# Agent attention with a PReLU MLP: the first batch's scores with agents as rows, in halves of TensorE's columns

## Chip, cores and metric

The kernel runs on one core of a Trainium2 chip. The metric is device time in microseconds; each kernel is run several times and the median is given. The engines are TensorE (PE in the profile), VectorE (DVE), ScalarE (ACT), GpSimd (POOL) and SyncE (SP), which issues the DMAs here.

## The reference

Agent attention for 2 batches of 12480 rows and 128 channels, with 49 agents, then an MLP of width 2048 with a learned slope for negative values:

```python
scale = 1.0 / np.sqrt(q.shape[-1])
def sm(a, b):
    s = scale * (a @ b.transpose(0, 2, 1))
    s = s - s.max(-1, keepdims=True)
    e = np.exp(s)
    return e / (e.sum(-1, keepdims=True) + 1e-09)
agent_v = sm(agents, k) @ v            # 49 x 128 per batch
x = sm(q, agents) @ agent_v            # 12480 x 128 per batch
h = x @ w_in                           # 24960 x 2048
out = (np.maximum(h, 0) + alpha * np.minimum(h, 0)) @ w_out
```

Everything is fp32. q, k and agents are drawn with a spread of 0.8, w_in and w_out arrive as fp64 and are put together from their two words on the chip.

## The kernel before

The work is in two parts. A first part handles batch 0's keys and values, w_in, w_out and the first queries. Then a long loop of 52 groups of 480 rows, 8 steps each, computes h (`g1`), its ReLU halves on ACT and DVE, and the output (`g2`), with batch 1's keys and values worked in between at fixed steps. `agent_v` is never formed for the loop: it is multiplied into w_in first (`fold_tasks`), and the loop multiplies query weights by that product (`sab`).

In the first part the keys come in blocks of 512, 25 in all, two blocks to a load. Per block `k_transpose_pe` transposes four 128x128 pieces on TensorE (tile ktp) and ACT copies them (kt). `k_logits` takes each piece as weights and the 49 agents as moving data, so scores lie with keys as rows, 49 columns per piece (kl); ACT copies them to an SBUF tile s (`k_take`, line 426). In five spans of blocks (`CUTS`) DVE takes the maximum over keys (`k_max_keys`, line 445); two transposes on TensorE turn it into one maximum per agent and spread it to all rows (`k_max_rows`, `k_max_spread`). Then `k_exp_a` (line 529) subtracts it on DVE or GpSimd, `k_exp` takes the exponential on ACT and `k_av` multiplies weights and values (av, line 561), with a column of ones next to each 128 values for the denominator. `k_factors` and `k_gather` bring the five spans to one maximum. The fold follows: `t1` divides by the denominator, `t2` transposes (avt), `ta` multiplies by w_in (a_ps) and splits the product into two parts.

What an engine does when is written out by step numbers: a plan from step to functions, walked in order, so each engine has one fixed list. Loads go out on SP's queue in the order of a sorted list, each when one of the 14 buffers of a ring is free; K, V, w_in and w_out share that ring. The first queries' chain (`q_transpose` to `q_split`; q_max, line 798, is a GpSimd all-reduce) is put among these steps by `CHAIN_0`, their loads by `Q_LOADS`. `stoke` issues dummy matmuls. `narrow` joins the fp64 words on DVE, partly on GpSimd, and `narrow_wo` makes the two parts of (1 - alpha) w_out.

## Time and profile before

| | |
|---|---|
| median of 3 runs | 1011.86 us (1010.86 to 1012.33) |
| the profiled execution's own time | 1012.12 us |
| its span | 1010.0 us |
| TensorE busy over the span | 994.7 us, 98% |
| DVE, ACT, GpSimd busy | 841.8, 631.0, 111.7 us |
| first matmul of the long loop | 84.72 us |

Times inside a trace count from the first instruction of the span; the profiled execution is 2.12 us longer than its span. Busy shares over the whole span hide the first part, so the table by stage matters more: 0 to 8.38 is the start, up to 73.30 the blocks, up to 79.87 the way to the fold, up to 84.72 the fold, and then the loop. An fp32 matmul appears as two records (two passes), an fp32r matmul as one; a shape as 64*128 means that only half of the array's rows are used, and two such matmuls on different halves stand side by side.

### The profile page before, as it was taken

The page shows a single profiled execution, that of the slowest core. Times are in us where ns is not written, and L with a number is a line of the kernel's source. Part 1 is how long each engine was busy: PE and PEld are TensorE (multiplying, and loading weights), DVE is VectorE, ACT ScalarE, POOL GpSimd, SP SyncE. Part 2 cuts the span into 40 slices and gives each one's busy share as a digit, 9 for nine tenths or more (in the row PEclk, how much of TensorE's full clock was granted, in tenths as well). Part 3 has the DMA queues.
Part 4 walks back from the last instruction along what each step waited for, and adds up shares of the span by engine and source line. Part 5 has one row for each costly group of instructions (what it writes and reads, how often), then busy time and mean ns, then how long its engine had stood idle before and what let it go on. Part 6 is the DMA issues. An engine that isn't in the chain of part 4 may idle for free.

```text
span 1010.0 us, 22035 instructions
## 1 busy us (share of the span) xinstructions
PE 994.7 (98%) x9154; PEld 898.9 (89%) x9154; DVE 841.8 (83%) x1058; ACT 631.0 (62%) x803; POOL 111.7 (11%) x106
## 2 busy tenths in 40 slices
PE   9998999999999999999999999999999999999997
PEld 7885899999998999999988888888888888888886
DVE  5966689889889999999997887888788878887775
ACT  5655555556557677677765666666666665666653
POOL 2430110110110110111011011101110111011100
PEclk9998999999999999999999999999999999999999
DMA  9970344444423432342322122122222222221101
GB/s 329 239 169 1 62 86 74 87 85 67 78 56 67 83 78 56 72 92 64 69 49 52 35 41 51 39 51 41 51 43 48 41 50 46 45 41 32 40 12 30
DMA packets 295764, 69.52 MB, mean 69 GB/s; under 512 B 263071, under 2 KB 290289, under 8 KB 295665
## 3 DMA queue, kind: packets, MB, share of 16 engines
q1 hardware_dynamic: 294673, 68.00, 32.4%
q8 instruction: 71, 1.16, 0.5%
q14 instruction: 28, 0.23, 0.1%
q10 hardware_dynamic: 992, 0.12, 0.1%
HBM read 42.59 MB, written 12.78 MB: 55 GB/s over the span
## 4 chain that ended last, share of the span: by engine, by line
PE 95%; DVE 2%; ACT 1%; POOL 0%; issue 0%; DVEq 0%; ACTq 0%; POOLq 0%
PE acc L894 55%; PE h L872 27%; PE kl L406 4%; PE lg L770 2%; PE acc L905 1%; PE av L594 1%; PE qsum L827 1%; PE av L561 1%; PE a_ps L656 1%; PE ktp L374 1%; PE warm L179 1%; PE lin_ps L723 0%; POOL qm L798 0%; DVE mx L445 0%; PE stoke L179 0%
## 5 line engine op out<-in xcount | busy, mean ns | idle before, releaser
L879 DVE SCALAR_TENSOR_TENSOR rl<-h,rh 128x960 fp32r<-128x960 f32 x416 | 478.8, 1151 | 128.3 <-ACT rh L878 125.6
L878 ACT ACTIVATE rh<-h 128x960 fp32r<-128x960 f32 x416 | 404.3, 972 | 276.5 <-PE h L872 269.4
L872 PE MATMUL h<-qmh,sab 64*128 64x480 f32 x1664 | 377.4, 378 | 0.5 <-DVE rl L879 0.5
L894 PE MATMUL acc<-rh,wl 64*128 64x480 f32 x1664 | 377.4, 379 | 0.0
L894 PE MATMUL acc<-rh,wh 64*128 64x480 f32 x1664 | 375.2, 377 | 0.0
L894 PE MATMUL acc<-rl,wh 64*128 64x480 f32 x1664 | 294.6, 378 | 0.0
L872 PEld LDWEIGHTS h<-qmh,sab 64*128 64x128 f32 x1664 | 233.1, 185 | 20.0 <-DVE rl L879 2.0
L894 PEld LDWEIGHTS acc<-rh,wl 64*128 64x128 f32 x1664 | 231.3, 184 | 18.1 <-issue 2.3
L894 PEld LDWEIGHTS acc<-rh,wh 64*128 64x128 f32 x1664 | 232.6, 185 | 16.2
L894 PEld LDWEIGHTS acc<-rl,wh 64*128 64x128 f32 x1664 | 199.7, 184 | 15.2
L872 PE MATMUL h<-qml,sab 64*128 64x480 f32 x832 | 204.1, 378 | 0.0
L798 POOL PARTITION_ALL_REDUCE qm<-qs x26 | 85.7, 3295 | 778.4 <-DVE qs L794 734.3
L872 PEld LDWEIGHTS h<-qml,sab 64*128 64x128 f32 x832 | 117.5, 185 | 7.0
L406 PEld LDWEIGHTS kl<-ag,kt 64*128 64x128 f32 (+2 forms) x588 | 49.3, 188 | 1.6 <-ACT s L535 0.7
L910 ACT COPY os<-acc 128x480 f32<-128x480 f32 x52 | 29.1, 560 | 34.3 <-PE acc L905 34.3
L406 PE MATMUL kl<-ag,kt 64*128 64x49 f32 (+2 forms) x588 | 49.9, 268 | 0.0
L807 ACT ACTIVATE qmh<-qs,padb 128x960 fp32r<-128x960 f32 x26 | 28.5, 1097 | 14.0 <-DVE qs L803 14.0
L911 DVE TENSOR_TENSOR os<-acc,os 128x480 f32<-128x480 f32 x52 | 34.0, 655 | 2.8 <-ACT os L910 2.4
L916 DVE STREAM_TRANSPOSE ot<-os 128x480 f32<-128x480 f32 x52 | 34.8, 669 | 0.0
L803 DVE TENSOR_TENSOR qs<-qs,qm 128x960 f32<-128x960 f32 x26 | 29.9, 1149 | 5.2 <-POOL qm L798 5.2
L921 DVE TENSOR_TENSOR ot<-ot,qr 128x480 f32<-128x480 f32 x52 | 33.7, 648 | 0.1
L794 DVE TENSOR_TENSOR qs<-qs,qw 128x960 f32<-128x960 f32 x26 | 29.9, 1149 | 1.2 <-DMA qw<-qs 1.1
(149 smaller groups left out, 850.6 us busy)
## 6 DMA issues: line engine op xcount, KB each, us to landing
qin<-in_q_dram SPq DMA_DIRECT2D x208, 60.0 KB
out_dram<-ot SPq DMA_DIRECT2D x206, 60.0 KB
qw<-qs SPq DMA_DIRECT2D x50, 240.0 KB
v<-in_v_dram SPq DMA_DIRECT2D x12, 512.0 KB
kb<-in_k_dram SPq DMA_DIRECT2D x96, 64.0 KB
v<-in_v_dram SPq DMA_DIRECT2D x24, 256.0 KB
k<-in_k_dram SPq DMA_DIRECT2D x11, 512.0 KB
win<-in_moe_w_in_dram SPq DMA_DIRECT2D x4, 512.0 KB
```

The lines of the kernel that those rows point to most:

```text
L406: nc.tensor.matmul(d[0:rows, c : c + NA], lhsT=kt[r0:r1, n * rows : (n + 1) * rows], rhs=st[b]["ag"][r0:r1, 0:NA], start=True, stop=True,)
L794: nc.vector.tensor_tensor(out=t, in0=t, in1=gq.pop(("w", k)), op=ALU.add)
L798: nc.gpsimd.partition_all_reduce(flat(t), flat(gq["s", k]), P, ReduceOp.max)
L803: nc.vector.tensor_tensor(out=t, in0=t, in1=gq.pop(("m", k)), op=ALU.subtract)
L872: nc.tensor.matmul(h[:, u, 0:GT], lhsT=w[a][r0:r1, f0 : f0 + P], rhs=x[r0:r1, :], start=n == 0, stop=n == 2,)
L878: nc.scalar.activation(out=rh, in_=h[:, :, 0:GT], func=AF.Relu)
L879: nc.vector.scalar_tensor_tensor(out=rl, in0=h[:, :, 0:GT], scalar=0.0, in1=rh, op0=ALU.max, op1=ALU.subtract)
L894: nc.tensor.matmul(acc[:, i, 0:GT], lhsT=a[r0:r1, 2 * m + u, :], rhs=x[r0:r1, u, :], start=m == 0 and n == 0, stop=False,)
L910: nc.scalar.copy(out=t, in_=acc[:, 0, 0:GT])
L911: nc.vector.tensor_tensor(out=t, in0=acc[:, 1, 0:GT], in1=t, op=ALU.add)
L916: nc.vector.transpose(out=t.rearrange("p t i -> p (t i)"), in_=oo.pop(g))
L921: nc.vector.tensor_tensor(out=t, in0=t, in1=gq.pop(("r", g)).to_broadcast([P, TB, 32]), op=ALU.mult)
```

## The change

Only batch 0's keys and values are worked differently; batch 1 and the loop stay. Keys come in packs of 1024 (a first one of 192 rows, then twelve), each one load; a pack's first 512 keys belong to half 0, the others to half 1. The 64 agent columns (49, padded) are the weights and 512 transposed keys the moving data, so `k_score` writes half 0 to PSUM rows 0 to 63 and half 1 to rows 64 to 127, which are two halves of the array's columns. Now a row is an agent: `k_top` keeps a running maximum per row on DVE, `k_weigh` takes the exponential of 512 scores straight from PSUM with the row sum, and a factor from the last maximum to this one; `k_back` transposes the weights back on TensorE, `k_mix` multiplies them by the values in halves of the columns again, and DVE adds to x with the factor. `k_merge` and `k_share` join the two halves and make the reciprocal of the denominator, which is now put on when the product with w_in is split (`take`). The column of ones, the score tile s, the spans and the GpSimd subtractions go. The ring has 12 buffers instead of 14, of 1024 words per partition instead of 1032. Two of the (1 - alpha) products move to GpSimd, `fold` and its like are made by DVE from the identity, and a small all-reduce on GpSimd (`library`) is called before the first queries'. Step numbers of the w_in and w_out slabs, the dummy matmuls (16 instead of 8), the query loads and the queries' chain are new.

```diff
-CHAIN_0 = (-9, -8, -7, -5, -4, -4, 0, 0, 3, 4, 6, 6)
+CHAIN_0 = (-19, -17, -15, -11, -9, -9, 0, 2, 8, 15, 18, 18)
...
+LAGS = (6, 8, 11, 17)
+LIBRARY_AT = 43
...
-Q_LOADS = (-21, -15)
+Q_LOADS = (-49, 0)
...
+    def library():
+
+        t = p2.tile([P, 1], F32, tag="none", name="none")
+        nc.gpsimd.partition_all_reduce(t, ones[:, 0:1].bitcast(F32), P, ReduceOp.max)
...
+    def load_wide(src, what, p):
+        r0, rows, nb = wide(p)
+        t = p_in.tile([P, RING], F32, tag="in", name=f"{what}w{p}")
+        view = t[0:rows, 0 : 2 * nb * C].rearrange("p (n c) -> p n c", c=C)
+        nc.sync.dma_start(
+            out=view, in_=src[0, r0 : r0 + rows * 2 * nb, :].rearrange("(p n) c -> p n c", p=rows)
+        )
+        kv[what, p] = view
+    def k_turn(p):
+        _, rows, nb = wide(p)
+        src, n = kv.pop(("k", p)), nb * rows
+        t = ps_h.tile([P, 2, 512], F32, tag="h", name=f"ktp{p}")
+        for i in range(2):
+            for j in range(nb):
+                nc.tensor.transpose(
+                    t[:, i, j * rows : (j + 1) * rows], src[:, i * nb + j, :],
+                    ident[0:rows, 0:rows],
+                )
+        kt = p_kt.tile([P, 2, KT], F32, tag="kt", name=f"ktw{p}")[:, :, 0:n]
+        nc.scalar.copy(out=kt, in_=t[:, :, 0:n])
+        kv["kt", p] = kt
+    def k_score(p):
+        kt = kv.pop(("kt", p))
+        n = kt.shape[2]
+        t = ps_a.tile([P, 512], F32, tag="acc", name=f"sc{p}")[:, 0:n]
+        for i, (r0, r1) in enumerate(TILES):
+            nc.tensor.matmul(t[r0:r1, :], lhsT=st[0]["ag"], rhs=kt[:, i, :], start=True, stop=True)
+        kv["sc", p] = t
+    def k_top(p):
+        w, t = st[0], kv["sc", p]
+        red = p2.tile([P, 1], F32, tag="red", name=f"red{p}")
+        nc.vector.tensor_reduce(out=red, in_=t, axis=AX.X, op=ALU.max)
+        if p == 0:
+            for x in ("nm", "den", "kf"):
+                w[x] = per_b.tile([P, NPK], F32, tag=x, name=x, bufs=1)
+            w["x"] = per_b.tile([P, C], F32, tag="xw", name="xw", bufs=1)
+            nc.vector.tensor_scalar(
+                out=w["nm"][:, 0:1], in0=red, scalar1=-SCALE, scalar2=None, op0=ALU.mult
+            )
         else:
+            nc.vector.scalar_tensor_tensor(
+                out=w["nm"][:, p : p + 1], in0=red, scalar=-SCALE, in1=w["nm"][:, p - 1 : p],
+                op0=ALU.mult, op1=ALU.min,
+            )
+    def k_weigh(p):
+        w, t = st[0], kv.pop(("sc", p))
+        e = p_e.tile([P, KT], F32, tag="e", name=f"ew{p}")[:, 0 : t.shape[1]]
+        nm = w["nm"][:, p : p + 1]
+        nc.scalar.activation(
+            out=e, in_=t, func=AF.Exp, bias=nm, scale=SCALE, accum_out=w["den"][:, p : p + 1]
+        )
+        if p:
+            nc.scalar.activation(
+                out=w["kf"][:, p : p + 1], in_=w["nm"][:, p - 1 : p], func=AF.Exp,
+                bias=nm, scale=-1.0,
+            )
+        kv["e", p] = e
+    def k_back(p):
+        _, rows, nb = wide(p)
+        e = kv.pop(("e", p))
+        t = ps_l.tile([P, 512], F32, tag="lg", name=f"etp{p}")
+        for j in range(nb):
+            nc.tensor.transpose(
+                t[0:rows, j * P : (j + 1) * P], e[:, j * rows : (j + 1) * rows], ident
+            )
+        et = p_e.tile([P, UB * P], F32, tag="et", name=f"et{p}")[0:rows, 0 : nb * P]
+        (nc.vector.tensor_copy if BACK_DVE[p] else nc.scalar.copy)(
+            out=et, in_=t[0:rows, 0 : nb * P]
+        )
+        kv["et", p] = et.rearrange("p (n a) -> p n a", a=P)
+    def k_mix(p):
+        w = st[0]
+        _, rows, nb = wide(p)
+        et, src = kv.pop(("et", p)), kv.pop(("v", p))
+        t = ps_k.tile([P, 512], F32, tag="km", name=f"avw{p}")[:, 0:C]
+        for j in range(nb):
+            for i, (r0, r1) in enumerate(TILES):
+                nc.tensor.matmul(
+                    t[r0:r1, :], lhsT=et[:, j, r0:r1], rhs=src[:, i * nb + j, :],
+                    start=j == 0, stop=j == nb - 1,
+                )
+        x = w["x"]
+        if p == 0:
+            nc.vector.tensor_copy(x, t)
+        else:
+            nc.vector.scalar_tensor_tensor(
+                out=x, in0=x, scalar=w["kf"][:, p : p + 1], in1=t, op0=ALU.mult, op1=ALU.add
+            )
+    def k_merge():
+        w = st[0]
+        last = w["nm"][:, NPK - 1 : NPK]
+        top = p2.tile([P, 1], F32, tag="red", name="top")
+        for i, (r0, r1) in enumerate(TILES):
+            o0, o1 = TILES[1 - i]
+            nc.scalar.copy(out=top[r0:r1, :], in_=last[o0:o1, :])
+        nc.vector.tensor_tensor(out=top, in0=top, in1=last, op=ALU.min)
+        f = per_b.tile([P, NPK], F32, tag="kff", name="kff", bufs=1)
+        nc.scalar.activation(out=f, in_=w["nm"], func=AF.Exp, bias=top, scale=-1.0)
+        w["fold"] = per_b.tile([P, P], F32, tag="foldw", name="foldw", bufs=1)
+        nc.vector.tensor_scalar(
+            out=w["fold"], in0=both, scalar1=f[:, NPK - 1 : NPK], scalar2=None, op0=ALU.mult
+        )
+        nc.vector.tensor_tensor(out=f, in0=f, in1=w["den"], op=ALU.mult)
+        den = p2.tile([P, 1], F32, tag="red", name="den_sum")
+        nc.vector.tensor_reduce(out=den, in_=f, axis=AX.X, op=ALU.add)
+        w["den_sum"] = den
+    def k_share():
+        w = st[0]
+        t = ps_l.tile([P, 512], F32, tag="lg", name="den_ps")[:, 0:1]
+        nc.tensor.matmul(t, lhsT=both, rhs=w.pop("den_sum"), start=True, stop=True)
+        rs = w["rs"] = per_b.tile([P, 1], F32, tag="rsw", name="rsw", bufs=1)
+        nc.vector.tensor_scalar(out=rs, in0=t, scalar1=1e-9, scalar2=None, op0=ALU.add)
+        nc.vector.reciprocal(out=rs, in_=rs)
...
+        def take(hi, lo, ps):
+            if b:
+                nc.scalar.copy(out=hi, in_=ps)
+                nc.vector.tensor_tensor(out=lo, in0=ps, in1=hi, op=ALU.subtract)
+            else:
+                rs = w["rs"][:, 0:1]
+                nc.scalar.activation(out=hi, in_=ps, func=AF.Copy, scale=rs)
+                nc.vector.scalar_tensor_tensor(
+                    out=lo, in0=ps, scalar=rs, in1=hi, op0=ALU.mult, op1=ALU.subtract
+                )
...
+        for p in range(NPK):
+            at(4 * p, k_turn, p)
+            loads.append((4 * p + LAGS[3] - V_AHEAD, load_wide, v, "v", p))
+            for n, f in zip(LAGS, ((k_score, k_top), (k_weigh,), (k_back,), (k_mix,))):
+                for g in f:
+                    at(4 * p + n, g, p)
+        q0 = 4 * NPK
+        end = q0 - 4 + LAGS[1]
+        at(end + 1, k_merge)
+        at(end + 2, k_share)
```

On TensorE, in the middle of the first part, two blocks of 512 keys before (ktp transposes, av values, kl scores):

```order
L374 MATMUL ktp0_20_671<-ident_82,k0_20_408 128x128 x4
L561 MATMUL av0_1_648<-v0_4_358,s0_173 49x129 x4
L406 MATMUL kl0_19_690<-ag0_165,kt0_19_643 128x49 x4
L374 MATMUL ktp0_21_696<-ident_82,k0_20_408 128x128 x4
L561 MATMUL av0_1_648<-v0_4_358,s0_173 49x129 x4
L406 MATMUL kl0_20_717<-ag0_165,kt0_20_676 128x49 x4
```

and a pack of 1024 keys now (avw values, sc scores, etp weights back, ktp keys):

```order
L434 MATMUL avw4_555<-vw4_372,et4_483 64x128 x8
L375 MATMUL sc7_569<-ktw7_500,ag0_160 64x512 x2
L417 MATMUL etp6_582<-ident_82,ew6_536 128x128 x4
L361 MATMUL ktp9_597<-ident_82,kw9_406 128x128 x8
L434 MATMUL avw5_610<-vw5_449,et5_531 64x128 x8
L375 MATMUL sc8_633<-ktw8_548,ag0_160 64x512 x2
```

Eight matmuls of 49 columns, eight of 129 and eight transposes have become two matmuls of 512 columns, eight of 128 and twelve transposes, of four different packs; the last two rows begin the next round.

On SP, around the second query load before (qin; k and v are packs of batch 0):

```order
L225 DMA wo_3_468<-in_moe_w_out_dram 128x4x256
L346 DMA k0_22_471<-in_k_dram 128x1024
L740 DMA qin1_486<-in_q_dram 32x15x32 x8
L346 DMA v0_8_495<-in_v_dram 128x8x128
L346 DMA k0_24_502<-in_k_dram 96x256
L346 DMA v0_10_552<-in_v_dram 128x8x128
```

and now, around the first (kw, vw are packs; win and wo are slabs of the weights):

```order
L349 DMA kw3_174<-in_k_dram 128x1024
L761 DMA qin0_176<-in_q_dram 32x15x32 x8
L234 DMA win_3_185<-in_moe_w_in_dram 128x1024
L349 DMA kw4_187<-in_k_dram 128x1024
L349 DMA vw0_189<-in_v_dram 96x256
L243 DMA wo_0_191<-in_moe_w_out_dram 128x4x256
L349 DMA kw5_193<-in_k_dram 128x1024
```

and the second:

```order
L349 DMA vw9_553<-in_v_dram 128x1024
L349 DMA vw10_565<-in_v_dram 128x1024
L349 DMA vw11_608<-in_v_dram 128x1024
L761 DMA qin1_620<-in_q_dram 32x15x32 x8
L349 DMA vw12_629<-in_v_dram 128x1024
L761 DMA qin2_1001<-in_q_dram 32x15x32 x8
```

The first query load has moved ahead of the last w_in slab and the fifth key pack, the second from the middle of the values to just ahead of the last value pack.

On DVE, at the end of the first part, before (x the weighted values, qs and qml the queries' scores and the lower part of their weights, avt the fold):

```order
L803 TENSOR_TENSOR qs0_866<-qs0_866,qm0_910 128x960
L504 COPY kfs0_948<-kf_ps0_942 49x5
L506 TENSOR_SCALAR x0_176<-x0_176,kfs0_948 49x129
L510 SCALAR_TENSOR_TENSOR x0_176<-x0_176,kfs0_948 49x129 x3
L816 TENSOR_TENSOR qml0_966<-qs0_866,qmh0_955 128x960
L573 SCALAR_TENSOR_TENSOR x0_176<-av0_4_937,kfs0_948,x0_176 49x129
L630 TENSOR_SCALAR rs0_1022<-x0_176 49x1
L633 RECIPROCAL rs0_1022<-rs0_1022 49x1
L634 TENSOR_TENSOR x0_176<-x0_176,rs0_1022 49x128
L647 COPY avt0_1028<-avt_ps0_1026 128x128
```

and now (nm the running minimum of negated maxima, top and kff the merge of the halves, rsw the reciprocal, wl a remainder of w_out, xw the weighted values):

```order
L454 TENSOR_TENSOR top_847<-top_847,nm_234 128x1
L458 TENSOR_SCALAR foldw_853<-both_85,kff_851 128x128
L461 TENSOR_TENSOR kff_851<-kff_851,den_235 128x13
L463 TENSOR_REDUCE den_sum_856<-kff_851 128x1
L472 TENSOR_SCALAR rsw_860<-den_ps_858 128x1
L473 RECIPROCAL rsw_860<-rsw_860 128x1
L320 TENSOR_TENSOR wl_97<-part3_788,wh_96 128x512
L824 TENSOR_TENSOR qs0_703<-qs0_703,qm0_824 128x960
L442 SCALAR_TENSOR_TENSOR xw_237<-xw_237,kf_236,avw11_872 128x128
L442 SCALAR_TENSOR_TENSOR xw_237<-xw_237,kf_236,avw12_882 128x128
L837 TENSOR_TENSOR qml0_895<-qs0_703,qmh0_892 128x960
L664 COPY avt0_951<-avt_ps0_949 128x128
```

The queries' subtraction stood ahead of the merge of the spans; now the merge of the halves and the reciprocal stand ahead of it, and the last two additions to x behind it.

## Rows read from the trace of the kernel before

**Rows 1.** Table by stage: us, busy per engine, TensorE's clock, DMA share, GB/s.

```profile
8.38:73.30 64.92, 63.36 (x527) 56.51 (x527) 49.11 (x97) 40.45 (x100) 25.60 (x46) 1.00 0.93 258
73.30:79.87 6.57, 2.19 (x18) 1.75 (x17) 4.54 (x11) 4.25 (x10) 0.78 (x1) 0.95 0.00 0
79.87:84.72 4.85, 4.46 (x6) 1.63 (x6) 1.27 (x3) 0.58 (x1) 0.00 (x0) 0.50 0.00 0
84.72:1010.00 925.28, 918.21 (x8591) 834.46 (x8590) 783.88 (x932) 584.46 (x691) 84.54 (x52) 1.00 0.29 55
```

**Rows 2.** Chain of waits, middle stage: start, duration, what, count.

```profile
13.96 1.23 PE stoke L179 x5
...
21.72 0.83 PE kl L406 x8
...
42.99 0.46 PE ktp L374 x4
43.44 1.02 PE av L561 x8
44.46 1.02 PE kl L406 x8
```

**Rows 3.** Chain of waits from 74 to 93 us.

```profile
74.11 1.17 DVE qs L803
...
75.31 1.10 ACT qmh L807
...
76.49 1.10 ACT qs L812
...
80.67 0.30 DVE avt L647
...
81.02 3.78 PE a_ps L656 x4
...
91.40 1.06 PE a_ps L656 x2
```

**Rows 4.** Timeline of GpSimd: start, duration, operation, idle before.

```profile
71.02 3.06 POOL L798 PARTITION_ALL_REDUCE qm<-qs  x1 [5.94 <-issue]
```

**Rows 5.** Timeline of TensorE, scores of the second batch.

```profile
141.75 1.97 PE L406 MATMUL kl<-ag,kt 64*128 64x49 f32 x31
...
143.55 0.27 PE L406 MATMUL kl<-ag,kt 64*128 64x49 f32 x1
```

**Rows 6.** Groups by line, 0 to 90 us, weight loads: busy us, mean ns.

```profile
L561 PEld LDWEIGHTS av<-v,s 128*49 128x49 f32 x192 | 20.4, 123 | 3.0 <-issue 1.6 <-ACT s L535 0.7 <-ACT aq L203 0.3
```

**Rows 7.** Groups by line, 0 to 90 us, DVE.

```profile
L445 DVE TENSOR_REDUCE mx<-s 128x49 f32<-128x1176 f32 x3 | 6.8, 2260 | 0.0
...
L445 DVE TENSOR_REDUCE mx<-s 128x49 f32<-128x588 f32 x2 | 2.4, 1178 | 0.0
...
L529 DVE TENSOR_TENSOR s<-s,kmax 128x196 f32<-128x196 f32 x6 | 2.1, 358 | 0.0
L663 DVE TENSOR_TENSOR sab<-a_ps,sab 128x512 fp32r<-128x512 f32 x3 | 2.1, 685 | 2.8 <-ACT sab L662 2.8
...
L264 DVE TENSOR_SCALAR scale_win<-mag_win 128x512 uint32<-128x512 uint32 x4 | 1.7, 423 | 0.0
...
L463 DVE TENSOR_REDUCE mcol<-mx_ps 49x1 f32<-49x128 f32 x5 | 1.4, 283 | 0.4 <-PE mx_ps L461 0.4
```

**Rows 8.** Groups by line, 0 to 90 us, ACT and GpSimd.

```profile
L378 ACT COPY kt<-ktp 128x512 f32<-128x512 f32 x24 | 14.1, 589 | 11.7 <-PE ktp L374 11.6
L529 POOL TENSOR_TENSOR s<-s,kmax 128x196 f32<-128x196 f32 x18 | 13.5, 770 | 8.9 <-DVE kmax L472 8.8
```

**Rows 9.** Table by stage, the loads of K and of V.

```profile
2.00:21.00 19.00, 18.12 (x114) 15.23 (x113) 11.11 (x35) 8.07 (x18) 4.04 (x10) 1.00 1.00 356
...
47.00:63.00 16.00, 15.92 (x129) 13.60 (x129) 12.81 (x22) 9.18 (x25) 8.46 (x13) 1.00 1.06 272
```

**Rows 10.** Timeline of SP: the first query load, eight issues.

```profile
21.05 9.35 SPq L740 DMA_DIRECT2D qin<-in_q_dram  x8
```

More of the change, by code (lines that the diff above doesn't have):

```diff
@@ L78 @@
     W = 512
-    N_IN = 14
+    N_IN = 12
     WARM = 13
-    RING = 2 * UB * (C + 1)
+    RING = 2 * UB * C
+    REST = N % (2 * KT)
+    NPK = N // (2 * KT) + 1
     NM = NF // 2
     SCALE = 1.0 / math.sqrt(C)
+    assert 0 < REST <= 2 * P and REST % 2 == 0
     assert N % GT == 0 and N % 64 == 0 and NA <= HALF and C == P and D == P and DFF % W == 0
@@ L112, in blocks, with wide @@
         return u * KT, n // nb, nb
+    def wide(p):
+        if p == 0:
+            return N - REST, REST // 2, 1
+        return (p - 1) * 2 * KT, P, UB
     ident = const.tile([P, P], F32, name="ident")
@@ L133 @@
     st = [
-        dict(rows=2 * NA, cols=2 * C + 2) if b else dict(rows=NA, cols=C + 1) for b in range(B)
+        dict(rows=2 * NA, cols=2 * C + 2) if b else {} for b in range(B)
     ]
@@ L156, in constants @@
         nc.gpsimd.memset(ones.bitcast(F32), 1.0)
-        for t, w in ((fold, HALF), (pair, NA)):
-            nc.gpsimd.memset(t, 0.0)
-            view = t.rearrange("p (h c) -> p h c", h=2)[:, :, 0:NA]
-            for base in (0, -NA):
-                nc.gpsimd.affine_select(
-                    out=view, in_=view, compare_op=ALU.not_equal, fill=1.0,
-                    base=base, pattern=[[0, 2], [-1, NA]], channel_multiplier=1,
-                )
+        for t, w, gap in ((fold, HALF, NA), (pair, NA, NA), (both, HALF, HALF)):
+            rows = t.shape[0]
+            if w > NA:
+                nc.gpsimd.memset(t, 0.0)
+            parts = [ident[0:rows, i : i + NA].unsqueeze(1) for i in (0, gap)]
+            v.tensor_tensor(
+                out=t.rearrange("p (h c) -> p h c", h=2)[:, :, 0:NA],
+                in0=parts[0].to_broadcast([rows, 2, NA]),
+                in1=parts[1].to_broadcast([rows, 2, NA]), op=ALU.add,
+            )
         valid = const.tile([P, 1], F32, name="valid")
@@ L320, in k_begin @@
         st[b]["x"] = per_b.tile(
[L321 removed]
+            [st[b]["rows"], 2, st[b]["cols"]], F32, tag=f"x{b}", name=f"x{b}", bufs=1
         )
[L324 to L325 removed]
     kv = {}
[L329 to L350 removed]
@@ L367, in load_blk @@
         return t
-    def k_transpose_pe(b, u):
-        _, rows, nb = blocks(u)
-        src = kv.pop(("k", b, u))
-        t = ps_h.tile([P, 2, 512], F32, tag="h", name=f"ktp{b}_{u}")[:, 0, 0 : nb * rows]
-        for n in range(nb):
-            nc.tensor.transpose(
-                t[:, n * rows : (n + 1) * rows], src[:, n, 0:C], ident[0:rows, 0:rows]
-            )
-        kt = p_kt.tile([P, KT], F32, tag="kt", name=f"kt{b}_{u}")[:, 0 : nb * rows]
-        nc.scalar.copy(out=kt, in_=t)
-        kv["kt", b, u] = kt
     def load_kb(b, u):
@@ L640, in t2 @@
             w["ps"] = pair_tile(f"avt_ps{b}")[:, 0, :]
-            for i in range(parts):
+            jobs = [(w["x"], w["fold"])] if b == 0 else [
+                (w["x"][:, i * C : (i + 1) * C], fold[0:rows, :]) for i in range(parts)
+            ]
+            for i, (x, f) in enumerate(jobs):
                 nc.tensor.matmul(
-                    w["ps"][:, 0:P], lhsT=w["x"][:, i * C : (i + 1) * C], rhs=fold[0:rows, :],
-                    start=(i == 0), stop=(i == parts - 1),
+                    w["ps"][:, 0:P], lhsT=x, rhs=f, start=i == 0, stop=i == len(jobs) - 1
                 )
@@ L661, in f @@
                     sl = slice(n * W, (n + 1) * W)
-                    nc.scalar.copy(out=w["sa"][:, sl], in_=ps[:, t, :])
-                    nc.vector.tensor_tensor(
-                        out=w["sb"][:, sl], in0=ps[:, t, :], in1=w["sa"][:, sl],
-                        op=ALU.subtract,
-                    )
+                    take(w["sa"][:, sl], w["sb"][:, sl], ps[:, t, :])
             return f
@@ L676, in ts @@
             w["zl"] = per_b.tile([P, D], F32R, tag="zl", name=f"zl{b}")
-            nc.scalar.copy(out=w["zh"], in_=w["z_ps"])
-            nc.vector.tensor_tensor(
-                out=w["zl"], in0=w["z_ps"], in1=w["zh"], op=ALU.subtract
-            )
+            take(w["zh"], w["zl"], w["z_ps"])
         whole = [(0, 1), (2, 3)] if b else [(n,) for n in range(4)]
-        first = [t1, t2] + [ta(*ns) for ns in whole]
+        first = [t1] * b + [t2] + [ta(*ns) for ns in whole]
         rest = [tz, ts]
@@ L996 @@
             at(q0 + j, f, 0)
+        at(LIBRARY_AT, library)
         for n in range(8):
```

222 lines of the change are left out of this document (43 added, 179 removed).

## The prediction

> **What bounds the kernel now.** Begin with the table by stage [rows 1]. From 84.72 us to the end (925.28 us) TensorE is busy 918.21 us at granted clock 1.00: the long loop is TensorE's. The change does not touch it, apart from the first fold in front of it, so I take its length as fixed. What can move is the time at which its first matmul, h of step 0, starts: 84.72 us. Before that stand three stages. From 8.38 to 73.30 the first batch's keys and values are worked off, with TensorE busy 63.36 of 64.92 us, DVE 49.11, ACT 40.45 and the DMA engines at 0.93. From 73.30 to 79.87 TensorE does 2.19 us of work. From 79.87 to 84.72 it runs at clock 0.50, its lower level of 1.2 GHz.
>
> The chain of waits [rows 2] shows the middle stage as TensorE work end to end: per 512 keys four transposes 0.46, scores 1.02 and values 1.02 us, so 5.0 us per 1024 keys; early blocks, without values, have scores of 0.83. So the stage is TensorE's too, though the DMA lane is nearly full. The tail [rows 3] hangs on another lane: GpSimd's maximum over the first queries ends at 74.09, then DVE subtracts, ACT takes two exponentials, and DVE, in its fixed order, comes to the value chain only behind them. GpSimd's maximum itself stood idle 5.94 us with nothing shown as its cause [rows 4].
>
> **The change on TensorE's lane.** A pack is 1024 keys, twelve and a small one.
> Transposes stay: 8 per pack, 0.91 us, 11.1 in all.
> Scores were 16 matmul records of 49 columns per 1024 keys (2.04 or 1.66 us). Now they are two matmuls of 512 columns into column halves, two passes each. A pass of 512 columns took 3.78/4 = 0.945 us at half clock [rows 3], so 0.47 at full: 1.89 us if the halves follow each other, 0.95 if they overlap fully. Passes go out in order (half 0 twice, then half 1 twice), so I allow one pass at each end alone: three slots, 1.4 us.
> Values were 16 records of 129 columns, 2.04 us. Now 16 passes of 128 columns: 2.04 one after the other (0.1275 each), 1.02 overlapped; with one pass alone 1.15.
> New: four transposes back, 0.46 us. Switching between whole array and halves: the a_ps pair at full clock, standing between matmuls in row halves, took 1.06 us against 2 x 0.47 [rows 3], so 0.115 for in and out, once per pack.
> So a pack is 0.91 + 1.4 + 0.46 + 1.15 + 0.1 = 4.0 us, against 5.0.
>
> No row shows column halves. The nearest are row halves: in the second batch, 32 score passes in halves took 143.55 - 141.75 = 1.80 us [rows 5], 0.056 each, where the first batch's whole-array passes took 0.83/8 = 0.104 [rows 2]. Two-pass fp32 matmuls in two halves did overlap. I therefore stand near the overlapped end and keep the serial one for the range.
>
> The Trainium skill's page "TensorEngine Tiling (Array Packing)", Key Properties, has tiles loading weights and multiplying independently, and says that changing the mode drains the engine; by the first the sum stands, and for the second the 0.115 us stands in. Its page "TensorE: Matmul & The Clock Gate", Measured speedup vs the span model, gives column tiles a gain within a few ns of row tiles. But the same page, Part 3, The mechanism, lets a weight load overlap a running matmul only when the row groups differ, and column halves share all rows; that speaks against the change and is the fourth case below. The value rows do not bear it out in the whole array: a pass took 0.1275 us with a weight load of 0.123 us beside it [rows 6].
>
> The lane: 11.1 transposes, 12 x 1.4 + 0.3 = 17.1 scores, 5.6 back, 14.0 values, 1.4 switches, 16 dummy matmuls at 1.23/5 = 0.246 [rows 2] = 3.9, query scores 0.9, small ones 0.4: 54.4 us, against 64.92. Without waiting it runs from 8.4 to 62.8; the last pack's scores, with 4.6 us of work behind them, end at S = 58.2.
>
> **DVE's lane.** Of 49.11 us go the key maxima and what hung on them: 9.1 (3 x 2.260 + 2 x 1.178), ten groups of small operations, the subtractions (2.1) the largest, 8.4 in all, and two 512-wide products moved to GpSimd, 1.4 [rows 7]. New are 13 row maxima over 512 scores. Their bounds are the 128-column maximum, 0.283, and the strided 588-element one, 1.178; I take the 512-wide operation on PSUM, 0.685. That makes 8.9; running minima 13 x 0.15, updates of x 12 x 0.34, three copies back 2.0, and the query subtraction that falls into the stage now, 1.2. Sum 47 us: no longer much shorter than TensorE's 54. In its list up to nine 512-wide operations stand between two row maxima: in the longest group, around the fifth pack, five at 0.423 and four at 0.685 [rows 7], with the maximum and small ones 6.4 us. That exceeds a pack's 4.0 by 2.4, and the exponential, the transpose back and TensorE wait for it. I add 2.4: S = 60.5. Without any idle DVE alone would put S at 55.5; with the share it is filled now (49.11/64.92 = 0.76) at 64.
>
> ACT, at 40.45 of 64.92 us, has room. Its 24 key copies of 0.589 [rows 8] become half as many of twice the width; copies of scores give way to copies of the weights turned back (ten of 512, 0.59 each), and 24 exponentials of 196 columns to 13 of up to 512. Even a third more would leave it under TensorE. GpSimd loses 13.5 us of subtractions [rows 8]. So neither decides.
>
> **Loads.** K ran at 356 GB/s; values, in 512 B pieces since a column of ones stood beside each row, at 272 [rows 9]. Now they have no such column. 14.9 MB at 356 are 42 us; two query loads, 0.49 MB each in 128 B pieces, I estimate at a third of that rate, 4 us each: about 50 us after the first issue, under 60. But SP took 9.35 us to issue a query load [rows 10]. The first now stands before the last slab of w_in and the fifth key pack: SP comes to that pack at about 14 us, and TensorE wants it, by its lane, at 19. The second stands before the last value pack. SP comes to it when a weight slab is done on DVE, some 16 us of TensorE work before that pack is used; 9.35 us of issue and 4 of transfer fit, with about 2 us to spare. If they didn't, the price would be what is missing.
>
> **The tail, from S.** Row maximum and minimum to S+0.9; exponential, factor, two swaps on ACT to 2.2; merge on DVE, ACT and DVE to 3.6; the sum over halves on TensorE 4.0; reciprocal, a weight remainder 0.69 and the query subtraction 1.16 to 6.3; two ACT exponentials, 1.10 each, to 8.6; DVE's split 1.16, to 9.8; the avt copy 0.3, 10.1; two a_ps 2.0, 12.1. The new wait is that of the sum over halves on TensorE: the last transposes back, two value packs and the 2.2 us of weight transposes are queued behind it for about 2 us, and end at about S+9, still beneath DVE's 9.8. So what is late next is again the query chain, held now by the merge ahead of it on DVE. The maximum on GpSimd is issued early, behind an early dummy call, and out of it; if that cover went, its 3.06 us [rows 4] would come back.
> h then starts at 60.5 + 12.1 = 72.6 at full clock. If the gaps here lower the clock as the one before 79.87 did, a_ps take 3.78 instead of 2.0: 74.4. I take 73.5, the middle. The gain is 84.72 - 73.5 = 11.2 us. The profiled execution took 1012.12 us, of which 1010.0 are span; that makes 1000.9. The median of the runs, 1011.86, is 0.26 lower: 1000.7.
>
> **The rivals.**
> *Lanes out of step.* DVE stays filled at 0.76 (S = 64) and TensorE, waiting more often, drops to 1.2 GHz at places: h at 76 to 80, time 1003 to 1008. For it: DVE is nearly as full as TensorE. Against: TensorE hardly idled in the stage before [rows 1].
> *Halves one after the other.* Scores 1.89, values 2.04: 1.38 us more per pack; S near 73, a tail of 13 since the value packs now end last, h at 86 to 89: 1013 to 1017, slower. It decides once scores and values of a pack take more than 2.55 + 11.2/12 = 3.5 us. Against it: the row halves overlap [rows 5].
> *Weight loads not hidden* by the other half. Values at 16 x 0.123 = 1.97 instead of 1.15, 9.8 us over 12 packs: about 1010.5.
> *Full overlap and DVE the bound*: S = 55.5, h at 67.6: 995.
>
> **Numbers.** Forecast 0.60 (own range 997 to 1004), out of step 0.16, serial 0.10, weight loads 0.07, DVE-bound 0.07. A change of 0.2% is 2.0 us, about what a measurement of this kernel can tell. Faster 0.84 (all but the next two), same 0.06 (most of the weight-load case), slower 0.10 (serial). The range 994 to 1010 leaves out the serial case and the outer edges.
>
> **What would show it.** Scores and values of a pack of 2.4 to 2.7 us on TensorE confirm the overlap; 3.9 refutes it. A pack every 4.0 to 4.5 us, h of step 0 between 69 and 78 us, and from there to the end again about 925 us confirm the sum. A last value pack that waits for DMA, a clock of 0.50 in the stage, or a loop longer than 927 us would make it wrong.

## The result and the profile after

The changed kernel takes 997.29 us (median of 4 runs, 997.11 to 999.15) against 1011.74 us in the same session (1010.86 to 1012.33): ratio 0.9862, 95% interval 0.9845 to 0.9879. Forecast were 1000.7 us with 994 to 1010 as the range. The profiled execution took 997.22 us, of which 995.4 are span.

The table by stage of the changed kernel, to be set beside [rows 1] (columns as there; the stages end where its own work ends):

```profile
8.38:13.56 5.18, 2.87 (x18) 1.85 (x18) 1.24 (x6) 2.45 (x4) 0.00 (x0) 1.00 1.07 321
13.56:18.00 4.44, 4.44 (x16) 2.38 (x17) 2.53 (x7) 1.44 (x3) 0.00 (x0) 0.62 0.81 122
18.00:60.00 42.00, 39.28 (x339) 26.00 (x339) 40.42 (x83) 34.53 (x74) 10.98 (x13) 1.00 0.97 338
60.00:64.33 4.33, 0.98 (x16) 0.77 (x17) 3.65 (x9) 1.65 (x6) 2.71 (x1) 1.00 0.71 109
64.33:73.98 9.65, 8.43 (x61) 6.10 (x61) 4.06 (x9) 5.63 (x12) 0.00 (x0) 0.82 0.01 2
73.98:995.40 921.42, 913.66 (x8591) 883.16 (x8590) 783.56 (x933) 584.61 (x691) 84.50 (x52) 1.00 0.30 55
```

Two things are to be seen. The loop begins at 73.98 us instead of 84.72, 10.74 us earlier (forecast 73.5). And the loop itself, which the prediction took as fixed at 925.28 us, takes 921.42: 3.86 us less. With 0.30 us less outside the span (1.82 instead of 2.12) that is the whole 14.9 us between the two profiled executions. From 18 to 60 us DVE is now the fullest engine, 40.42 of 42.00.

TensorE's timeline of the changed kernel, one pack and the way to the loop (start, duration, engine, line, operation, count, and in brackets idle time and what ended it); it answers to [rows 2, 3]:

```profile
51.52 1.03 PE L375 MATMUL sc<-ktw,ag 128*64 128x512 f32 x4
52.82 0.66 PE L417 MATMUL etp<-ident,ew 128*128 128x128 f32 x4 [0.28 <-ACT ew L401]
53.31 1.04 PE L361 MATMUL ktp<-ident,kw 128*128 128x128 f32 x8
54.28 1.09 PE L434 MATMUL avw<-vw,et 128*64 128x128 f32 x16
55.21 1.03 PE L375 MATMUL sc<-ktw,ag 128*64 128x512 f32 x4
...
58.05 1.03 PE L375 MATMUL sc<-ktw,ag 128*64 128x512 f32 x4
59.31 0.65 PE L417 MATMUL etp<-ident,ew 128*128 128x128 f32 x4 [0.23 <-ACT ew L401]
59.89 1.09 PE L434 MATMUL avw<-vw,et 128*64 128x128 f32 x16
64.33 0.35 PE L470 MATMUL den_ps<-den_sum,both 128*128 128x1 f32 x2 [3.35 <-DVE den_sum L463]
65.03 0.76 PE L417 MATMUL etp<-ident,ew 128*128 128x128 f32 x4 [0.34 <-DVE rsw L472]
65.72 1.98 PE L434 MATMUL avw<-vw,et 128*64 128x128 f32 x16
68.19 1.37 PE L434 MATMUL avw<-vw,et 128*64 128x128 f32 x16 [0.50 <-ACT qmh L828]
69.49 1.97 PE L719 MATMUL turn<-ident,win 128*128 128x128 f32 x16
71.30 0.39 PE L660 MATMUL avt_ps<-foldw,xw 128*128 128x128 f32 x2
72.06 1.98 PE L684 MATMUL a_ps<-win,avt 128*128 128x512 f32 x4 [0.38 <-DVE avt L664]
...
73.98 0.48 PE L893 MATMUL h<-qmh,sab 64*128 64x480 f32 x2
```

From start to start a pack's values cost 0.93 us (54.28 to 55.21), its transposes 0.97, the transposes back 0.49; four score passes last 1.03. The lines show the sum over halves waiting 3.35 us for DVE, and then 1.98 and 1.37 us for values that take 1.09 elsewhere: after the gap the granted clock falls from 1.00 to 0.50 (1.2 GHz), where it is from 66 to 68 us, and is back at 1.00 (2.4 GHz) from 69 us on; from 64.33 to the start of the loop that is 0.82 on average.

DVE and GpSimd in the same tail, from two timelines of the changed kernel:

```profile
59.61 0.68 DVE L382 TENSOR_REDUCE red<-sc 128x1 f32<-128x512 f32 x1
60.33 1.11 DVE L391 SCALAR_TENSOR_TENSOR nm<-red,nm 128x1 f32<-128x1 f32 x1
61.37 0.68 DVE L421 COPY et<-etp 128x512 f32<-128x512 f32 x1
61.97 0.68 DVE L320 TENSOR_TENSOR wl<-part,wh 128x512 fp32r<-128x512 f32 x1
```

```profile
49.84 0.38 POOL L190 PARTITION_ALL_REDUCE none<-ones  x1 [6.21 <-issue]
59.64 3.07 POOL L819 PARTITION_ALL_REDUCE qm<-qs  x1 [2.64 <-DVE qs L815]
```

The last running minimum (`nm`) takes 1.11 us while GpSimd's maximum runs; most of its fellows take 0.16. The idle time that stood before that maximum [rows 4] now stands before the early dummy call and has gone from the maximum itself.

### The profile page after: what moved, and what is told of

Read it like the earlier page. It is cut to its first block, busy times and chain, and to the rows that moved or that the text cites. A ratio compares the mean times of both kernels' runs of the same rounds, so it can differ in the third digit from the quotient of the medians.

```text
span 995.4 us, 21785 instructions
## 1 busy us (share of the span) xinstructions
PE 976.1 (98%) x9049; PEld 924.8 (93%) x9049; DVE 838.9 (84%) x1063; ACT 631.6 (63%) x791; POOL 99.1 (10%) x74
## 4 chain that ended last, share of the span: by engine, by line
PE 93%; DVE 3%; ACT 1%; DMA 1%; issue 1%; DVEq 0%; ACTq 0%
PE acc L915 55%; PE h L893 27%; PE lg L791 2%; PE kl L513 2%; PE acc L926 2%; PE av L611 1%; PE qsum L848 1%; DMA vw<-in_v_dram 1%; PE a_ps L684 1%; PE warm L197 1%; ACT ktw L366 0%; DVE red L382 0%; PE lin_ps L744 0%; DVE nm L391 0%; ACT ew L401 0%
## 5 line engine op out<-in xcount | busy, mean ns | idle before, releaser
L893 PE MATMUL h<-qmh,sab 64*128 64x480 f32 x1664 | 390.5, 377 | 0.9 <-DVE lin L734 0.8
L915 PE MATMUL acc<-rh,wl 64*128 64x480 f32 x1664 | 391.1, 378 | 0.0
L915 PE MATMUL acc<-rh,wh 64*128 64x480 f32 x1664 | 389.1, 376 | 0.0
L915 PE MATMUL acc<-rl,wh 64*128 64x480 f32 x1664 | 303.3, 377 | 0.0
L915 PEld LDWEIGHTS acc<-rh,wl 64*128 64x128 f32 x1664 | 238.2, 184 | 7.1 <-issue 2.5
L915 PEld LDWEIGHTS acc<-rh,wh 64*128 64x128 f32 x1664 | 238.7, 184 | 3.7
L915 PEld LDWEIGHTS acc<-rl,wh 64*128 64x128 f32 x1664 | 213.2, 185 | 4.2
L893 PE MATMUL h<-qml,sab 64*128 64x480 f32 x832 | 212.5, 376 | 0.0
L769 DVE STREAM_TRANSPOSE qt<-qin 128x960 f32<-128x960 f32 x26 | 30.4, 1168 | 0.0
L781 DVE TENSOR_TENSOR ql<-qt,qh 128x960 fp32r<-128x960 f32 x26 | 29.9, 1148 | 0.0
```

What stands on the lines that cost most here:

```text
L769: nc.vector.transpose(out=flat(t), in_=gq.pop(("in", k)).rearrange("p h t i -> p (h t i)"))
L781: nc.vector.tensor_tensor(out=t, in0=gq.pop(("t", k)), in1=gq["h", k], op=ALU.subtract)
L893: nc.tensor.matmul(h[:, u, 0:GT], lhsT=w[a][r0:r1, f0 : f0 + P], rhs=x[r0:r1, :], start=n == 0, stop=n == 2,)
L915: nc.tensor.matmul(acc[:, i, 0:GT], lhsT=a[r0:r1, 2 * m + u, :], rhs=x[r0:r1, u, :], start=m == 0 and n == 0, stop=False,)
```

## Experiments

The text under each edit is what stood on record before the run. Where a median is of several runs, it is beside before in the same session.

### One half's values after the other's

```diff
-        for j in range(nb):
-            for i, (r0, r1) in enumerate(TILES):
+        for i, (r0, r1) in enumerate(TILES):
+            for j in range(nb):
```

> The changed kernel with one edit: in k_mix the eight matmuls of half 0 come first and the eight of half 1 after them, instead of in turn; same work, same result. Theory (the halves' overlap is what pays): a pack's values go from 0.93 us to about 1.9 on TensorE, 0.95 x 12 = 11 us more on its lane, h of step 0 from 73.98 to 82 to 85 us, total from 997.3 to 1005 to 1008. Rival (DVE or DMA holds the stage and TensorE has slack): values 1.9 too, but h of step 0 moves by less than 3 us, total 997 to 1000. Third (the overlap doesn't hang on the order): values stay 0.93 and nothing moves.

Measured 999.96 us (998.93 to 1000.55), ratio 0.9871 (0.9836 to 0.9907); loop from 76.75 us, 921.45 long. One pack in its TensorE timeline:

```profile
56.68 1.25 PE L434 MATMUL avw<-vw,et 128*64 128x128 f32 x13
57.66 0.64 PE L375 MATMUL sc<-ktw,ag 128*64 128x512 f32 x1
57.77 0.49 PE L434 MATMUL avw<-vw,et 128*64 128x128 f32 x3
58.09 1.02 PE L375 MATMUL sc<-ktw,ag 128*64 128x512 f32 x3
59.05 0.66 PE L417 MATMUL etp<-ident,ew 128*128 128x128 f32 x4
```

From the first value to the scores of half 1 it is 1.41 us instead of 0.93; the first score pass of half 0 (57.66) already runs under the last values of half 1. With the scores that makes 2.37 us (56.68 to 59.05) against 0.93 + 0.96 (the scores from 40.27 to 41.23 us in the changed kernel, where nothing is waited for). So alternating from matmul to matmul is worth about 0.5 us per pack. The first theory had expected values of 1.9; at 1.41 they are still well below the 2.04 of the kernel before, so more than half of that gain does not hang on the alternation. What that part comes from, no run isolates. The loop begins 2.77 us later, which is what the rival expected, and not 12 x 0.5 = 5.8: TensorE had some 3 us of slack. Its waits for the exponential, 1.5 us up to 60 us in the changed kernel, are gone here.

### The loop's operands back at their old addresses

```diff
-    N_IN = 12
+    N_IN = 11
+        per_b.tile([P, HALF], F32, tag="ag", name="ag_first")
+        nc.gpsimd.memset(big(0, "first", F32)[:, 0:1], 0.0)
+        per_b.tile([P, 1000], F32, tag="room", name="room", bufs=1)
...
```

With tiles of unused room wh, wl, sab, qmh, qml, rh and rl stand where the kernel before had them.

> The changed kernel with unused tiles put in, so that all operands of the long loop (sab, qmh, qml, rh, rl, wh, wl, os, ot) lie at the SBUF addresses that they have in the kernel before; the ring has 11 buffers instead of 12, to make room; instruction order on TensorE is the same. Question: the loop took 921.42 us after and 925.28 before. Theory (addresses): the loop goes back to about 925, total 1001. Rival (it is something else, the time at which the loop starts or the place of the code): loop 921 to 922, total 997 to 998; a ring short by one buffer may cost the first part up to 1 us in either case.

Measured 1002.57 us (1001.87 to 1004.29), ratio 0.9901 (0.9864 to 0.9937). The loop in its table by windows:

```profile
74.47:1000.60 926.13, 918.68 (x8591) 889.98 (x8590) 785.00 (x933) 585.05 (x691) 84.49 (x52) 1.00 0.29 55
```

The same instructions in the same order on TensorE, the same clock, and 4.7 us more. So the loop's gain came from where the tiles lie in SBUF, as the first theory has it, though the loop came out 0.85 us longer than the 925.28 before.

### Which operand

Three kernels move one group each, and a fourth moves the relu halves by 96 B only.

```diff
-    both = const.tile([P, P], F32, name="both")
+    both = per_b.tile([P, P], F32, tag="both", name="both", bufs=1)
```

> The changed kernel with one 512 B tile (the 128 x 128 sum-over-halves matrix) taken from ahead of the weights to behind them: w_out's halves wh and wl stand 512 B lower, where they stood in the kernel before; every other operand of the loop keeps its address. Theory A, the weights' address decides: the loop (h of step 0 to the end) takes about 926 us instead of 921.4. Theory B, the address of the relu halves or of the fold's halves decides: 921 to 922. Theory C, the 4.7 us are a sum of small shares: 922.5 to 924. h of step 0 stays at 74 in all three.

```diff
+        room.tile([P, 1240], F32, name="room")
         p3 = ctx.enter_context(tc.tile_pool(name="p3", bufs=3))
```

> The changed kernel with 4960 B of unused room ahead of the pool of the relu halves: rh and rl stand at the addresses that they had in the kernel before, all other loop operands as in the changed one. Theory A, their address decides (they are the moving operand of 24 of a step's 36 matmuls passes, and ACT and DVE write them while TensorE reads others): loop about 926 us. Theory B, another operand decides: 921 to 922. Theory C, shares: 922.5 to 924.

```diff
+        nc.gpsimd.memset(big(0, "first", F32)[:, 0:1], 0.0)
         load_wide(k, "k", 0)
```

> The changed kernel with the two big buffers (the fold's halves sa, sb of both batches, 19.6 KB per partition each) put ahead of the small tiles, at the addresses of the kernel before; all else as in the changed one. Theory A, the fold's address decides (the weights of the twelve h passes of a step): loop about 926 us. Theory B, another operand decides: 921 to 922. Theory C, shares: 922.5 to 924.

```diff
+        room.tile([P, 24], F32, name="room")
         p3 = ctx.enter_context(tc.tile_pool(name="p3", bufs=3))
```

> The changed kernel with only 96 B of unused room ahead of the pool of the relu halves: rh begins at a multiple of 256 B (154112) as in the kernel before, instead of 160 B above one, but stays within 96 B of where the changed kernel has it. Theory A, the low part of the address decides (how a row of 480 values lies over blocks of up to 256 B): loop about 925 us as with the shift of 4960 B (924.9). Theory B, the place in the buffer at large decides: 921 to 922, as in the changed kernel.

The loop of each by windows, in this order:

```profile
73.86:995.30 921.44, 913.64 (x8591) 879.63 (x8590) 783.59 (x933) 584.58 (x691) 84.50 (x52) 1.00 0.30 55
```

```profile
74.16:999.10 924.94, 917.09 (x8591) 886.72 (x8590) 784.47 (x933) 585.08 (x691) 84.52 (x52) 1.00 0.30 55
```

```profile
73.63:995.90 922.27, 914.51 (x8591) 836.79 (x8590) 784.21 (x933) 584.76 (x691) 84.53 (x52) 1.00 0.30 55
```

```profile
74.58:999.50 924.92, 917.13 (x8591) 867.50 (x8590) 784.71 (x933) 585.39 (x691) 84.51 (x52) 1.00 0.30 55
```

Moving w_out's halves by 512 B does nothing (921.44), the fold's old place costs 0.9 us, the relu halves' pool 3.5; together 4.4 of the 4.7. The shift by 96 B costs as much as the one by 4960 B (19 x 256 + 96), so the low part of the address decides, not the place at large. Since 512 B leave the low part as it was, the weights' low part is not tested; nor were the query weights (qmh, qml) moved alone. The relu halves' pool holds the second batch's value tiles too, and the pool behind it moves along; that rh and rl are meant is an inference from their use in every step. Each of the four was run once, but the length of the loop repeats well: in the traces of eight kernels that leave the relu halves where the changed kernel has them, and the fold within 32 B of its place, it lies between 921.28 and 921.85.

### The kernel before, with 160 B of room

```diff
+        room = ctx.enter_context(tc.tile_pool(name="room", bufs=1))
+        room.tile([P, 40], F32, name="room")
         p3 = ctx.enter_context(tc.tile_pool(name="p3", bufs=3))
```

> The kernel before, unchanged but for 160 B of unused room ahead of the pool of the relu halves: rh and rl begin 160 B above a multiple of 256 B, as they do in the changed kernel. If the low part of this address is what shortened the loop, the loop takes about 921.8 instead of 925.3 us with h of step 0 still at 84.7, and the time falls by 3.5 us to about 1008.3 (ratio 0.9965). If the gain needs another operand of the changed kernel as well, the loop stays at 924.5 to 925.5 and the time within 1 us of before.

Measured 1008.55 us (1007.74 to 1009.98) against 1013.25, ratio 0.9960 (0.9944 to 0.9977).

```profile
84.80:1006.50 921.70, 914.58 (x8591) 872.04 (x8590) 782.72 (x932) 584.52 (x691) 84.58 (x52) 1.00 0.29 55
```

The old kernel gets the short loop, 921.70 us instead of 925.28, from an unused tile alone. The first theory held. The fold stands at its old place here, and no 0.9 us are to be seen for it; so that share, from one run, does not carry over.

### The tail

The weight transposes of the fold are put into the gap before the sum over halves:

```diff
+        at(end + 1, lin_turn, 0)
+        at(end + 1, lin_turn, 1)
...
-        for n in range(2):
-            lin_turn(n)
```

> The changed kernel with one edit: the sixteen transposes of w_in (lin_turn) stand ahead of the denominator's matmul on TensorE, in the gap of 3.35 us there, instead of behind the last values. Theory (the gap drops the clock and that sets the tail): TensorE works through the gap, granted clock stays 1.00 from 60 to 74 us, the last two packs' values take 0.93 each instead of 1.98 and 1.37, avt follows them at once, h of step 0 comes 1.5 to 2.5 us earlier, total 995 to 996. Rival (DVE's order, the query subtraction and split ahead of the avt copy, sets the tail): clock full, but h of step 0 within 0.7 us of 73.98, total 996.6 to 998.

996.33 us (996.07 to 996.75), ratio 0.9837 (0.9795 to 0.9879); loop from 73.03 us. The gap shrank from 3.35 to 1.46 us and both value packs ran in 1.09, but a_ps then waited 1.30 us for DVE, and ran 2.77. The loop began 0.95 us earlier, between the two expectations, and the ratio is not told apart from the changed kernel's. The next kernel also takes DVE's split behind the avt copy:

```diff
-        for j, f in zip(CHAIN_0, q_chain[:12]):
+        for j, f in zip(CHAIN_0, q_chain[:11]):
...
         t2()
+        q_split(0)
```

> As the run with the transposes in the gap, and the split of the first query weights (q_split, 1.15 us on DVE) comes behind the avt copy instead of ahead of it. Theory (both hold the tail): avt copy at about 68, a_ps at 68 to 70, h of step 0 at 70 to 71, total 993 to 994.5. Rival (ACT's two query exponentials, which end at 69.05, and the split of the first product hold it anyway): h of step 0 no more than 0.5 us earlier than with the transposes alone.

994.65 us (994.17 to 996.34), ratio 0.9823 (0.9787 to 0.9859). Its traced execution is the longest of its four (996.34), so it stands for the median badly: loop from 72.75 us, granted clock 0.61 from 64.2 to 68.2. The interval still overlaps the changed kernel's. Then the sum over halves goes behind the last but one value pack, and DVE's copies of turned weights to ACT:

```diff
-BACK_DVE = (0, 0, 0, 1, 0, 0, 0, 0, 1, 0, 0, 1, 0)
+BACK_DVE = (0, 0, 0, 0, 0, 0, 0, 0, 0, 0, 0, 0, 0)
...
-        at(end + 2, k_share)
+        at(end + 6, k_share)
```

> The kernel with the weight transposes in the gap and the split behind the avt copy, and on top: the three copies of weights turned back that DVE had go to ACT, and the sum over halves on TensorE moves behind the last transpose back and the last but one value pack. Theory A, DVE's list is what the end of the stage and the tail wait for (18.1 to 60 us: DVE busy 40.4 of 42): 2 us less on DVE, of which 0.7 us between the last maximum and the merge; TensorE's gap before the sum shrinks below 1 us, a_ps end by about 69.5, h of step 0 at 70 to 71.5 instead of 72.75, median 992 to 993.5. Theory B, TensorE and the loads hold the stage as much as DVE does, and ACT, with the three copies, is late for the exponentials: h at 72.5 to 74, 994.5 to 996.

995.24 us (995.14 to 995.86), ratio 0.9827 (0.9807 to 0.9847); loop from 71.94 us. The tail became shorter, 10.95 us from the last scores' end to the loop instead of 14.9, with clock 1.00 throughout; but those scores ended at 61.0 instead of 59.1. ACT's timeline of this kernel shows why:

```profile
50.87 0.59 ACT L421 COPY et<-etp 128x512 f32<-128x512 f32 x1 [0.69 <-PE etp L417]
51.36 0.96 ACT L800 COPY qs<-lg 128x960 f32<-128x960 f32 x1
52.33 1.92 ACT L809 COPY qw<-lg 64x960 f32<-64x960 f32 x2
54.28 0.69 ACT L401 ACTIVATE ew<-sc,nm 128x512 f32<-128x512 f32 x1
```

The exponential's minimum was ready at 51.6, but three query copies stood ahead of it, and TensorE waited 1.57 us. In the changed kernel they stand there too and end at 51.97; here they end at 54.25, behind a copy of turned weights that DVE had before and that waited 0.69 us for TensorE. So two copies go back to DVE:

```diff
-BACK_DVE = (0, 0, 0, 0, 0, 0, 0, 0, 0, 0, 0, 0, 0)
+BACK_DVE = (0, 0, 0, 1, 0, 0, 0, 0, 1, 0, 0, 0, 0)
```

> The kernel with the sum over halves behind the last but one value pack, with only the last of DVE's three copies of weights turned back on ACT; the other two go back to DVE. Theory A, the two early copies made ACT late for the exponentials (TensorE waited 1.57 us for one at 53.5 to 55.1): without them the last pack's scores end at 59 instead of 61.0 us, the tail stays at 11.0 to 11.5, h of step 0 comes at 70 to 71, median 992.5 to 994. Theory B, the later end of the stage has another cause (the order of DVE's list or the loads): h at 71.5 to 72.5, 994.5 to 995.5.

In the trace this came out as the first theory has it: last scores end at 59.1, loop from 70.91 us, profiled execution 994.50 us; only the tail, 11.8 us, is a little longer than its 11.0 to 11.5. The median of four is 995.43 (994.50 to 996.34), outside what it expected, with ratio 0.9823 (0.9808 to 0.9837). That is faster than the changed kernel (0.9862, 0.9845 to 0.9879), but not told apart from the kernel with the split moved, which has the same ratio. Three microseconds less in the trace's first part did not all reach the medians; why the other executions are up to 1.8 us longer was not traced.

### The first query load later

```diff
-Q_LOADS = (-49, 0)
+Q_LOADS = (-37, 0)
```

> The changed kernel with the first query load twelve steps (three packs) later in the order of loads. Theory A, the early query load slows the first loads: TensorE's 2.2 us of idle time before 13.56 us and the clock of 0.62 from there to 18.0 (4.4 x 0.38 = 1.7 us) go, h of step 0 comes at 70 to 72 instead of 74.0, median 993.5 to 995.5. Theory B, its 10.3 us of issue on SP then hold key and value loads back in the middle of the stage, TensorE waits there for about as much: h at 73 to 76, 996 to 999. Theory C, the early idle time and low clock have nothing to do with the query load and stay: h at 73.5 to 74.5, 997.

997.38 us (996.71 to 998.88), ratio 0.9853 (0.9836 to 0.9869), loop from 74.12 us. The third theory's time, though not its mechanism. The clock from 13.56 to 18.0 us was 1.00, while the idle time before it stayed (TensorE busy 2.99 of 5.18 us). The end of the stage on TensorE:

```profile
57.01 1.03 PE L375 MATMUL sc<-ktw,ag 128*64 128x512 f32 x4
...
63.30 0.56 PE L470 MATMUL den_ps<-den_sum,both 128*128 128x1 f32 x2 [3.34 <-DVE den_sum L463]
64.19 1.09 PE L417 MATMUL etp<-ident,ew 128*128 128x128 f32 x4 [0.34 <-DVE rsw L472]
65.21 1.98 PE L434 MATMUL avw<-vw,et 128*64 128x128 f32 x16
67.69 1.98 PE L434 MATMUL avw<-vw,et 128*64 128x128 f32 x16 [0.50 <-issue]
69.59 2.01 PE L719 MATMUL turn<-ident,win 128*128 128x128 f32 x16
```

The last scores and the sum over halves come 1.0 us earlier than in the changed kernel (58.0 and 63.30 against 59.1 and 64.33). But the clock is 0.50 from 64 to 68 us, both value packs take 1.98 and the weight transposes begin at 69.59, against 69.49: what was gained in the stage was lost again to the clock behind the gap. Three kernels with the load in its old place show the same pair: with the relu halves moved by 4960 or 96 B, and with all operands moved, the clock from 13.56 us was 1.00, the last scores ended at 58.5 to 58.6, the clock behind the gap was 0.50 from 64 to 68 us, and the loop began at 74.16 to 74.58. So the clock from 13.56 us varies without the load, and about half of the microsecond may be the load's.

## Why the prediction held, and where not

**Halves overlap.** The step held. Two value passes in halves cost 0.93/8 = 0.116 us, no more than one alone (0.1275 in the whole array); with the halves one after the other it was 1.41 in all, so they do overlap, though part of the gain on 2.04 has another source. Scores were given three slots, 1.4 us, for their order; four passes last 1.03 us, two passes of 0.47 [rows 3] and little more, so the two halves ran side by side almost from end to end: the term is 0.4 too long. Values were 1.15, and took 0.93. A pack costs 0.93 + 0.97 + 0.49 + about 1.0 = 3.4 us of TensorE, not 4.0. So both marks set for the overlap were passed on the fast side: scores and values 1.9 us and not 2.4 to 2.7, a pack every 3.7 us on average (21.24 to 58.05) and not every 4.0 to 4.5. The serial rival falls, and so does that of weight loads not hidden: sixteen loads of 0.123 us [rows 6] one after the other would not fit into 0.93.

**The lanes.** S was forecast at 60.5 and came at 59.1. With TensorE's terms 0.6 us too long per pack, it would have come earlier if TensorE alone had set it; the slack of 3 us in the run with the values in turn, and the chain of waits speak for DVE, as the rival with full overlap had it. From 47.95 to 61.46 us the chain is DVE's list end to end:

```profile
47.95 0.41 DVE scale_wo L282
...
59.70 0.61 DVE red L382
60.33 1.12 DVE nm L391
```

That rival put S at 55.5 by a sum of 47 us without idle time. Neither number holds: the text's own terms add up to 48.3, and DVE was busy for 43.3 us from 8.38 to 59.10 and idle for 7.4, 5.85 of them before 18 us. (The 64 of the first rival does not come out of its terms either: 47 us at a share of 0.76 end at 70.) Of the 43.3, some 3.3 are operations that stretch beside GpSimd, which the sum lacked. DVE and GpSimd in the changed kernel:

```profile
23.93 0.74 DVE L391 SCALAR_TENSOR_TENSOR nm<-red,nm 128x1 f32<-128x1 f32 x1
26.64 0.68 DVE L391 SCALAR_TENSOR_TENSOR nm<-red,nm 128x1 f32<-128x1 f32 x1
42.61 1.30 DVE L267 TENSOR_SCALAR mag_wo<-mag_wo 128x512 f32<-128x512 f32 x1
```

```profile
23.38 1.28 POOL L294 TENSOR_TENSOR win<-mag_win,win 128x512 f32<-128x512 f32 x1 [1.90 <-DVE win L287]
26.02 1.28 POOL L294 TENSOR_TENSOR win<-mag_win,win 128x512 f32<-128x512 f32 x1 [1.37 <-DVE win L287]
41.59 2.04 POOL L311 TENSOR_TENSOR part<-wo,oma 128x512 f32<-128x512 f32 x2
```

The two minima end within 0.02 us of GpSimd's addition (24.67 and 24.66, 27.32 and 27.30), the third operation 0.28 us behind GpSimd's products. Five such operations before S, three minima and two of 512 values, are 3.3 us over their usual 0.16 and 0.43. The Trainium skill's page "SBUF — State Buffer", section "Who interferes with whom", says that a DVE instruction with two SBUF inputs contends with a GpSimd instruction that reads SBUF, and that the lock on the ports they share is exclusive; the minima agree, for `nm` has two such inputs, while the two operations of 512 values have one and are not covered by it. No run took GpSimd's operation away, but the other kernels moved the start of the minimum against it. Two of them, the one with the values in turn and the one with the sum over halves later:

```profile
62.83 0.39 DVE L391 SCALAR_TENSOR_TENSOR nm<-red,nm 128x1 f32<-128x1 f32 x1
61.76 0.77 DVE L391 SCALAR_TENSOR_TENSOR nm<-red,nm 128x1 f32<-128x1 f32 x1
```

Beside GpSimd's maximum the last minimum takes 0.39, 0.77 or 1.11 us, and in every kernel with the new first part it ends 1.79 to 1.81 us after that maximum begins (61.42 and 60.73 in these two, 59.64 in the changed one). So GpSimd's operation holds it, though not for the whole 3.07 us: in the changed kernel a remainder of w_out (`wl`, also two SBUF inputs) runs its usual 0.68 at 61.97, with the maximum still going.

**The tail.** Forecast 13.0 us, measured 14.9 (59.1 to 73.98). Its step "what is late next is again the query chain" failed: the list on DVE made the merge late first, with the minimum of 1.11, a copy and a weight remainder ahead of it, so that the sum over halves began at S+5.2 and not S+3.6. It stood 3.35 us on TensorE with two value packs and the transposes of w_in queued behind it, which the text had put beneath DVE's split at S+9.8; they ended at S+12.2. DVE's split, itself kept waiting by those value packs, ended at 71.01, 0.3 us before the transposes. The clock did fall in that gap, as the upper of the two cases had it, but it was the values that ran slow, and a_ps ran at full clock. Transposes in the gap alone brought the loop 0.95 us forward; with the split, the last copy and the place of the sum changed too, the tail is 11.8 us at full clock. That bears out the wait on TensorE as a part of the tail, without giving each edit its share.

**The loop.** The step that failed: "the change does not touch it ... I take its length as fixed". It is 3.86 us shorter, more than the whole miss of 3.4 us. The tiles that the change adds and removes shift every pool behind them, and 96 B of shift are worth 3.5 us over 416 steps, 8.4 ns per step. That it is the place of the relu halves' pool and of what lies behind it is shown in both kernels; through which access it costs time is open. The mark set for this, "a loop longer than 927 us", looked to one side only. Another mark, a clock of 0.50 in the stage, did appear, from 14.5 to 17.5 us; by the kernels without it, it cost S some 0.5 us and the start of the loop nothing.

**The sum.** Start of the loop 0.5 us later than forecast (1.4 earlier in S, 1.9 longer in the tail), loop 3.86 shorter, 0.30 less outside the span: 1000.9 - 3.7 = 997.2. The errors in the first part cancelled, which is luck: without the loop's gift the forecast would have been met within 0.2 us, for a partly wrong reason.

**Loads.** No value pack waited for DMA and keys did once, for 0.7 us; all loads together ran at 338 GB/s from 18 to 60 us, near the 356 assumed. But the 14.9 MB of the forecast are too few: keys and values are 12.8 MB, w_in and w_out 2.1 each, 17.0 in all, which by the forecast's own rates are 56 us and not 50. SP took 10.29 and 11.76 us to issue the two query loads, not 9.35. The DMA share of 0.97 says that there was little to spare.
